# Another order of work in the attention of an attention and two mixture-of-experts kernel, 32-column logits, weights loaded in order of use

## The chip, the cores and the metric

The kernel runs on one core of a Trainium2 chip. The metric is the device time of one execution in microseconds; lower is better. A run before gives the median of three executions.

## The reference, cut to what matters

Local attention in a band of seven keys plus attention over averages of four tokens, then a soft mixture of experts (every slot is a softmax over all tokens), then a top-2 mixture. Only the first two are touched by the change.

```python
B, H, S, D = 4, 8, 576, 64                       # attention, factor 4
q_d, k_d, v_d = means over 4 tokens of q, k, v
out_up = repeat(softmax(q_d @ k_d.T / 8) @ v_d, 4 times along S)
scores = where(|i - j| < 4, q @ k.T / 8, -1e9)
x = out_up + softmax(scores) @ v                 # -> (2304, 512)

logits = x @ phi                                 # 2304 x 32, 8 experts of 4 slots
d = softmax of logits over the tokens
slot_input = d.T @ x                             # 32 x 512
slot_out[e] = relu(slot_input[e] @ w1[e]) @ w2[e]   # w1 512x1024, w2 1024x512, fp32
x = (softmax of logits over the slots) @ slot_out
# then a noisy top-2 mixture of 8 experts on x
```

## The kernel before

**Attention (to 164 us of the trace).** The work is cut into 16 units, a unit being one batch and two heads. It is software-pipelined by hand: the loop over `p` from -1 to 14 runs through the names of `SEQ` (L21) once per period, and each name is a function with an offset, so that a period holds the scores of one unit, the outputs of the unit before it, the logits of the one before that and the loads of the next. On every engine the instructions stand in just this order; nothing reorders them. After the loop `TSEQ` (L23) does the last unit and the softmax of the slots. In a period TensorE does, with the name in `SEQ` ahead: `S` band scores (L285 adds the mask with one bf16 matmul, L289 twenty 64x35 matmuls), `CP` transposes of the probabilities (L375), `SD` the scores of averages (L300), `CD` their transposes (L386), `A0`/`A1` transposes of the next unit's k and q (L231), `VD` averages of v (L268, L272), `DP` band output (L414), `EP` transposes of the output (L441, L443), `LG` logits (L463 and L465, the second one 64-column matmul for the last 64 tokens), `DD` output of the averages (L421). Every fp32 matmul shows as two records in the trace.

PSUM is read by ScalarE (ACT) or VectorE (DVE): `cp` (L216) takes DVE for the names in `ON_V`, ACT for the others. `a0j`/`a1hj` are k and q of the next unit, `pig` the transposed band probabilities (tile `PT`), `d0`/`d1` those of the averages (`PdT`), `v0`/`v1` the averaged values (`Vd`), `x0`/`x1` the band output of even and odd groups (`xT`), `k0`/`k1` its transposes (`xK`). `XA` (L433) adds the output of the averages, which stands in the same PSUM bank as the odd groups that `x1` reads. GpSimd (POOL) averages k (`KD`) and half of q (`DQ0`, L249 and L251); DVE sums the other half (`DQ1`, L245). POOL also normalises `P` and `Ed` (`P0`, `P1`, `DM`).

**Soft experts (164 to 199 us).** `hidden(e)` (L795) multiplies the slots by w1[e], `hidden_t` (L807) transposes the result by two full transposes, `second(e)` (L817) multiplies by w2[e]. The sixteen 2 MB matrices come over SP's queue (L101), each as two halves of four 256 KB or two 512 KB transfers: eight during attention (`W` issues one half a period, two in the first), three in the tail (`R2`), and the last five into ring slots that come free as the first ones are used. They are loaded in the order of their numbers, 0 (w1[0]), 1 (w2[0]), 2 (w1[1]) and so on.

Behind that stand the routing (to 215 us) and the top-2 mixture (to 492 us), which the change leaves alone. `hot(n)` (L543) issues n bf16 matmuls of 128x512 whose result nobody reads; `H2` and `H1` in `TSEQ` call it.

Of the kernel before, what the change touches and what calls it, by code (L numbers as in the profile page):

```python
# [18 lines left out]
SEQ = """S SK CP EP01 ld EP10 M EP00 ST SD CD z EP11 ED0 EL SS MD A0 ED1 EX a00 W a01 SU SU_ A1 P1 a100 a101  # L19
a110 a111 P0 KD DQ0 VD z DP V0 V1 DQ1 DX EP LG DD x1 LA lV x0 X1 SE RD DM X0 XA""".split()  # L20
TSEQ = """S:15 CP:14 W EP01:14 EP00:14 SD:15 M:15 EL:15 EP10:14 EX:15 EP11:14 CD:14 ED0:14 MD:15 SU:15 VD:14 DP:14 V0:14 V1:14 EP:13  # L21
# [12 lines left out]
N2 = 3  # L34


@with_exitstack
def attn_moe_moe_kernel(ctx: ExitStack, tc: tile.TileContext, q, k, v, moe_phi, moe_w1, moe_w2,
# [51 lines left out]
    phi4 = const.tile([128, 4, 4 * NS], F32, name="phi4")  # L90
    wgn = const.tile([128, 4, 2 * E], F32, name="wgn")

    def wload(src, kk, pool=ringa, names=("wr", "wr")):

        n = kk // 2
        ts = [pool.tile([128, 2048], F32, name=nm).rearrange("p (k f) -> p k f", k=n) for nm in names]
        sv = src.rearrange("(k p) f -> p k f", p=128)

        def go(i, eng=nc.sync):
            for k in range(n):  # L100
                eng.dma_start(out=ts[i][:, k:k + 1], in_=sv[:, n * i + k:n * i + k + 1])  # L101
        return lambda k: ts[k // n][:, k % n], [lambda i=i, **k: go(i, **k) for i in range(len(names))]
# [12 lines left out]
    with ExitStack() as tctx:  # L115
# [34 lines left out]
        P = a2.tile([128, NG, 64], F32, name="P")  # L150
        Vs = [(a1, a2)[i].tile([128, 5, 2, D], F32, name=f"V{i}") for i in range(2)]
# [27 lines left out]
        LD, VQ, KD, DQ, SD, SS, PD, PL, XL, XT, XK = ({} for _ in range(11))  # L179
# [81 lines left out]
        def v_pe(u):  # L261
# [12 lines left out]
            VQ[u] = (None, wk.tile([128, 2, 128], F32, name="Vd", bufs=1))  # L274

        def v_evac(u, i):
            xl, Vd = XL[u], VQ[u][1]
            if i:
                cp("v1", Vd[0:16, 1].rearrange("p (h d) -> p h d", h=2), xl[0:16, :, 434:498])
            else:  # L280
                cp("v0", Vd[:, 0], xl[:, 0, 290:418])

        def b_s(u):
            s = ps.tile([128, 512], F32, name="S")
            nc.tensor.matmul(s[:, 0:NG * KW], idb, mask.rearrange("p g k -> p (g k)"), start=True, stop=True)  # L285
# [6 lines left out]
            SS[u] = s  # L292
# [87 lines left out]
        def c_d(u):  # L380
# [8 lines left out]
            PdT = wk.tile([128, 2, 2, 144], F32, name="PdT", bufs=1)  # L389
            CT[u, 1] = (PdT, tt)  # L390
# [8 lines left out]
        def c_ed(u, kb):  # L399
            PdT, tt = CT[u, 1]  # L400
# [36 lines left out]
        def e_pe(u):  # L437
# [21 lines left out]
        def logit_pe(u, t2=None):  # L459
            xT, kk = XT[u], u % 4  # L460
            L = (ET_[u][1] if t2 is None else t2)[:, 128:320]
            for t in range(4):
                nc.tensor.matmul(L[32 * t:32 * t + 32, 0:128], phi4[:, kk, 0:NS], xT[:, 128 * t:128 * t + 128],  # L463
                                 start=True, stop=True, skip_group_check=True)
            nc.tensor.matmul(L[:, 128:192], phi4[:, kk], xT[:, 512:576], start=True, stop=True, skip_group_check=True)  # L465
# [79 lines left out]
        def ok(u):  # L545
# [8 lines left out]
              "DX": (soft_d2, 0, ()), "RD": (soft_d3, 0, ()), "DM": (soft_dm, 0, ()), "CP": (c_p, 1, ()),  # L554
# [23 lines left out]
        for i in range(NPRE):  # L578
            mload(i, ringa if i < 3 else ringb)
# [6 lines left out]
        for p in range(-1, NU - 1):  # L586
            if p == 0:
                nc.sync.dma_start(out=phi4[:, :, 0:NS], in_=moe_phi.rearrange("(k p) s -> p k s", p=128))
# [6 lines left out]
            for nm in SEQ:  # L595
# [66 lines left out]
        def slot_in():  # L662
            t = tp()
            for kk in range(4):
# [6 lines left out]
              "LG:15": lambda: logit_pe(NU - 1, tp()), "W": flush}  # L671
# [43 lines left out]
    with ExitStack() as mctx:  # L715
# [4 lines left out]
        for i in range(NPRE + N2, 2 * E):  # L720
            mload(i, ringa if i < NPRE + N2 + 3 else ringb)
# [79 lines left out]
        def hidden_t(e):  # L801
# [3 lines left out]
            ht_ = ps.tile([128, 2, 4, NS], F32, name="ht", bufs=1)  # L805
            for c in range(2):
                nc.tensor.transpose(ht_[:, c].rearrange("p j s -> p (j s)"), hs_[:, 128 * c:128 * c + 128], idf)  # L807
            nc.vector.tensor_scalar(hz[e][:, :, :, SPE * e:SPE * e + SPE], ht_[:, :, :, SPE * e:SPE * e + SPE],
                                    0.0, None, op0=ALU.max)
# [593 lines left out]
```

## Time and profile before

| what | us |
|---|---|
| runs, median of three | 496.54 (495.12, 496.54, 497.39) |
| the profiled execution's own time | 494.55 |
| its span in the trace | 492.7 |
| of that: start, before the first full period | 0 to 24.7 |
| thirteen periods, the regular ones of 8.3 to 8.8, those with a batch's slots of 10 | 24.7 to 141.6 |
| last unit and slots' softmax | 141.6 to 164.4 |
| soft experts | 164.4 to 198.8 |
| routing and top-2 mixture | 198.8 to 492.7 |

The profiled execution is 1.85 us longer than its span and 1.99 us below the median of the runs. A sum of terms worked out in the trace is therefore a time of that execution, and the median stands about 2 us above it.

### The profile page before, as it was taken

The page shows a single profiled execution, that of the slowest core. Times are in us where ns is not written, and L with a number is a line of the kernel's source. Part 1 is how long each engine was busy: PE and PEld are TensorE (multiplying, and loading weights), DVE is VectorE, ACT ScalarE, POOL GpSimd, SP SyncE. Part 2 cuts the span into 40 slices and gives each one's busy share as a digit, 9 for nine tenths or more (in the row PEclk, how much of TensorE's full clock was granted, in tenths as well). Part 3 has the DMA queues.
Part 4 walks back from the last instruction along what each step waited for, and adds up shares of the span by engine and source line. Part 5 has one row for each costly group of instructions (what it writes and reads, how often), then busy time and mean ns, then how long its engine had stood idle before and what let it go on. Part 6 is the DMA issues. An engine that isn't in the chain of part 4 may idle for free.

```text
span 492.7 us, 12033 instructions
## 1 busy us (share of the span) xinstructions
PE 470.2 (95%) x4569; PEld 355.9 (72%) x4569; DVE 277.4 (56%) x720; ACT 263.4 (53%) x698; POOL 199.2 (40%) x289
## 2 busy tenths in 40 slices
PE   5999999899998999899999999999999999999993
PEld 4688877777875543467787787887887887878882
DVE  7878877777875321696579545273462544624300
ACT  2567766666775021486365465483664746727410
POOL 5565636536540100166566677422222221222222
PEclk9999999999999799999999999999999999999997
DMA  9999998989979599999988744699958856333333
GB/s 160 278 243 214 233 221 192 242 216 202 265 239 345 171 393 399 389 346 338 365 258 228 224 75 76 150 363 297 275 72 229 216 128 154 43 45 43 45 43 46
DMA packets 108423, 104.16 MB, mean 211 GB/s; under 512 B 68170, under 2 KB 78090, under 8 KB 108362
## 3 DMA queue, kind: packets, MB, share of 16 engines
q1 hardware_dynamic: 101450, 90.50, 61.2%
q0 software_dynamic: 6912, 12.85, 16.6%
q8 instruction: 38, 0.62, 0.5%
q14 instruction: 23, 0.19, 0.1%
HBM read 83.60 MB, written 19.73 MB: 210 GB/s over the span
## 4 chain that ended last, share of the span: by engine, by line
PE 73%; issue 9%; DMA 7%; DVE 3%; POOL 2%; ACT 2%; POOLq 2%; SPq 0%; ACTq 0%; DVEq 0%
PE y L1054 34%; DMA wr<-in_moe_w_dram 5%; PE S L289 4%; PE t L231 3%; PE gx L871 3%; PE xl L421 3%; PE Sd L300 3%; PE xl L414 2%; PE t L375 2%; PE xl L268 2%; PE t L441 2%; PE h L1034 2%; PE t L386 2%; POOL out_dram L1073 2%; POOLq L1079 1%
## 5 line engine op out<-in xcount | busy, mean ns | idle before, releaser
L1054 PE MATMUL y<-whi,hl 128*128 128x512 f32 x320 | 127.3, 398 | 0.0
L1054 PE MATMUL y<-whi,hh 128*128 128x512 f32 x320 | 126.7, 396 | 0.4 <-ACT hh L1035 0.4
L1054 PE MATMUL y<-wlo,hh 128*128 128x512 f32 x320 | 126.5, 395 | 0.0
L1073 POOL DMA_INDIRECT out_dram<-ys,idx x40 | 64.5, 1612 | 107.9 <-ACT ys L1065 56.3
L1065 ACT ACTIVATE ys<-y,gt 128x512 f32<-128x512 f32 x40 | 27.4, 686 | 82.4 <-issue 46.9
L1026 DVE TENSOR_TENSOR wlo<-wr,whi 128x512 fp32r<-128x512 f32 x64 | 42.0, 692 | 50.3 <-ACT whi L1023 49.9
L1054 PEld LDWEIGHTS y<-wlo,hh 128*128 128x128 f32 x320 | 60.1, 188 | 12.9 <-issue 1.0
L1054 PEld LDWEIGHTS y<-whi,hl 128*128 128x128 f32 x320 | 60.1, 188 | 12.3 <-issue 2.1
L1054 PEld LDWEIGHTS y<-whi,hh 128*128 128x128 f32 x320 | 60.2, 188 | 11.8 <-ACT hh L1035 0.6
L333 POOL TENSOR_TENSOR P<-El,su 64x350 f32<-64x350 f32 x31 | 23.9, 772 | 59.7 <-DVE su L326 38.3
L1036 DVE SCALAR_TENSOR_TENSOR hl<-h,hh 128x256 fp32r<-128x256 f32 (+1 forms) x64 | 31.3, 489 | 16.0 <-ACT hh L1035 14.7
L1000 POOL DMA_INDIRECT tab<-stk,pos x36 | 35.6, 990 | 11.5 <-issue 10.7
L1036 DVE SCALAR_TENSOR_TENSOR hl<-gx,hh 128x256 fp32r<-128x256 f32 (+1 forms) x64 | 31.2, 487 | 10.7 <-ACT hh L1035 9.1
L1023 ACT ACTIVATE whi<-wr 128x512 fp32r<-128x512 f32 x64 | 36.9, 625 | 0.2
L1035 ACT ACTIVATE hh<-gx 128x256 fp32r<-128x256 f32 (+1 forms) x64 | 28.1, 439 | 15.0 <-PE gx L1034 12.5
L1035 ACT ACTIVATE hh<-h 128x256 fp32r<-128x256 f32 (+1 forms) x64 | 28.0, 437 | 12.5 <-PE h L1034 10.2
L1072 POOL MEMSET spacer<- 1x1 f32 x40 | 13.6, 340 | 41.6 <-issue 41.6
L219 ACT ACTIVATE PT<-t 64x256 f32<-64x256 f32 (+1 forms) x50 | 20.6, 417 | 13.5 <-PE t L375 12.7
L919 DVE TENSOR_TENSOR oh<-iot,R 128x256 fp32r<-128x256 f32 (+2 forms) x50 | 20.3, 439 | 11.4 <-PE xs L937 9.6
L231 PE MATMUL t<-idf,ld 96*128 96x96 f32 x192 | 21.1, 259 | 4.9 <-DMA ld<-in_k_dram 4.3
L219 ACT ACTIVATE xT<-xl 128x290 f32<-128x290 f32 x32 | 11.5, 411 | 26.2 <-PE xl L421 24.1
L289 PE MATMUL S<-K,Q 128*64 128x35 f32 x640 | 23.1, 231 | 2.2 <-issue 1.4
(301 smaller groups left out, 837.8 us busy)
## 6 DMA issues: line engine op xcount, KB each, us to landing
wr<-in_moe_w_dram SPq DMA_DIRECT2D x120, 256.0 KB, 5.6
wr<-in_moe_w_dram SPq DMA_DIRECT2D x56, 512.0 KB, 7.1
out_dram<-zero SPq DMA_DIRECT2D x20, 256.0 KB, 3.4
V<-in_v_dram SPq DMA_DIRECT2D x62, 80.0 KB, 5.2
ld<-in_k_dram SPq DMA_DIRECT2D x32, 144.0 KB, 4.7
ld<-in_q_dram SPq DMA_DIRECT2D x32, 144.0 KB, 4.4
XT<-tab SPq DMA_DIRECT2D x5, 320.0 KB, 5.6
tab<-zero SPq DMA_DIRECT2D x6, 256.0 KB, 4.8
```

The lines of the kernel that those rows point to most:

```text
L219: nc.scalar.activation(dst, src, AF.Copy)
L231: nc.tensor.transpose(t[:, 96 * c:96 * c + 96], ld[:, i, 3 * j + c].rearrange("p h d -> p (h d)"), idf[0:96, 0:96])
L289: nc.tensor.matmul(s[64 * a:64 * a + 64, KW * g:KW * g + KW], Q[:, c0:c0 + 32].rearrange("p i h -> p (i h)"), K[:, c0:c0 + KW], start=Fals ...
L333: eng.tensor_tensor(P[as_, :, HQ * a:HQ * a + KW], El[as_], su[as_, :, None].to_broadcast([64, NG, KW]), op=ALU.mult)
L1000: st = nc.gpsimd.indirect_dma_start(out=tab, out_offset=bass.IndirectOffsetOnAxis(ap=pos[:, c, i:i + 1], axis=0), in_=stk[:, i].bitcast(F3 ...
L1023: nc.scalar.activation(whi[:, kk], wb(kk), AF.Copy)
L1026: eng.tensor_tensor(wlo[:, kk], wb(kk), whi[:, kk].bitcast(F32), op=ALU.subtract)
L1035: nc.scalar.activation(hh[:, f], h, AF.Relu)
L1036: nc.vector.scalar_tensor_tensor(hl[:, f], h, 0.0, hh[:, f].bitcast(F32), op0=ALU.max, op1=ALU.subtract)
L1054: nc.tensor.matmul(y, l[:, kk, ts_], r_[:, kk], start=(m == 0), stop=(m == 23))
L1065: nc.scalar.activation(ys, YS.pop((e, ti)), AF.Copy, scale=gt[:, ti:ti + 1])
L1073: st = nc.gpsimd.indirect_dma_start(out=out, out_offset=bass.IndirectOffsetOnAxis(ap=idx[:, ti:ti + 1], axis=0), in_=ys, in_offset=None, c ...
```

## The change

- `SEQ` is another order, and `DM` works one unit later. The logits' second part becomes four 32-column matmuls like the first (so `phi4`, the copies of phi side by side, goes), and in the loop they are written into the bank of the scores (`SB`) instead of the transposes' bank.
- The mask's matmul becomes two of 64 columns. `Vd` and `PdT` are kept over the units with their second half zeroed, so that all four matmuls of `DD` take 128 rows.
- `ON_V` has other names, `DQ1` is done on POOL but for the last unit, and two `H2` (four spinning matmuls) and some other places in `TSEQ` are new.
- The sixteen matrices are loaded in `ORDW`, the order in which they are used; one half a period throughout; the last one (number 15) in another order of its quarters, the rows of `second`'s first pass first. `hidden_t` is eight matmuls of 32 columns.

```diff
-SEQ = """S SK CP EP01 ld EP10 M EP00 ST SD CD z EP11 ED0 EL SS MD A0 ED1 EX a00 W a01 SU SU_ A1 P1 a100 a101
-a110 a111 P0 KD DQ0 VD z DP V0 V1 DQ1 DX EP LG DD x1 LA lV x0 X1 SE RD DM X0 XA""".split()
+SEQ = """S ld DM M A0 a00 a01 A1 a110 a101 a100 EL SD a111 SK ST CP MD VD EP11 SS EP01 EP00 V0 EP10 V1 SU_ KD LG LA EX CD
+DQ1 W EP DP lV ED0 DX x1 ED1 DD x0 X0 X1 DQ0 SE SU P0 RD P1 XA""".split()
...
-LA:15 SE:3 X1:14 MT M4 SK:2 X1:15 SS:3 ST:3 MB R2 QW QS UA DN UB H1 SI H2 SK:3""".split()
+LA:15 SE:3 X1:14 SK:2 H2 MT M4 X1:15 SS:3 H2 ST:3 MB R2 QW QS UA DN UB H1 SI H2 SK:3""".split()
...
-ON_V = ['a110', 'a111', 'p00', 'v0', 'v1']
+ON_V = ['p11', 'k1', 'd1', 'a100', 'v0']
...
-NW = [2] + [1] * 14
+NW = [1] * 15
...
+ORDW = (0, 2, 1, 4, 3, 6, 5, 8, 7, 10, 9, 12, 11, 14, 13, 15)
...
-            if h:
+            if h and u == NU - 1:
                 return nc.vector.tensor_reduce(out=Dq[hs, :, h], in_=Q[hs, 0:576, h].rearrange(
...
-            nc.tensor.matmul(s[:, 0:NG * KW], idb, mask.rearrange("p g k -> p (g k)"), start=True, stop=True)
+            for a in range(2):
+                as_ = slice(64 * a, 64 * a + 64)
+                nc.tensor.matmul(s[as_, 0:NG * KW], idb[:, as_], mask.rearrange("p g k -> p (g k)"), start=True, stop=True,
+                                 skip_group_check=True)
...
-            xl, PdT, Vd = XL[u], CT[u, 1][0], VQ.pop(u)[1]
-            for kb, n in enumerate((128, 16)):
+            xl = XL[u]
+            for kb in range(2):
                 for h in range(2):
-                    nc.tensor.matmul(xl[64 * h:64 * h + 64, 1, 290:434], Vd[0:n, kb, 64 * h:64 * h + 64], PdT[0:n, kb, h],
+                    nc.tensor.matmul(xl[64 * h:64 * h + 64, 1, 290:434], Vd[:, kb, 64 * h:64 * h + 64], PdT[:, kb, h],
...
-            L = (ET_[u][1] if t2 is None else t2)[:, 128:320]
+            L = SB[u + 2][:, 0:192] if not TAIL else ET_[u][1][:, 128:320] if u in ET_ else tp()[:, 0:192]
...
-            nc.tensor.matmul(L[:, 128:192], phi4[:, kk], xT[:, 512:576], start=True, stop=True, skip_group_check=True)
+            for t in range(4):
+                nc.tensor.matmul(L[32 * t:32 * t + 32, 128:192], phi[:, kk], xT[:, 512:576], start=True, stop=True,
+                                 skip_group_check=True)
...
+            if i == 2 * E - 1:
+                go = [lambda f=f, c=c: f(ks=(c, c + 2)) for c in range(2) for f in go]
...
                 if p == -1 and nm == "lV":
                     nc.gpsimd.memset(PT, 0.0)
+                    nc.gpsimd.memset(Vd[:, 1], 0.0)
+                    nc.gpsimd.memset(PdT[:, 1], 0.0)
...
             for c in range(2):
-                nc.tensor.transpose(ht_[:, c].rearrange("p j s -> p (j s)"), hs_[:, 128 * c:128 * c + 128], idf)
...
+                for j in range(4):
+                    nc.tensor.matmul(ht_[32 * j:32 * j + 32, c], hs_[:, 128 * c + 32 * j:128 * c + 32 * j + 32], own_,
+                                     start=True, stop=True, skip_group_check=True)
```

The order of TensorE's instructions in a regular period, first before. The period runs from one `S` to the next; the names are tiles, `V_133` one of the two buffers of v.

```order
L285 LDWEIGHTS idb
L285 MATMUL S<-mask,idb 128x350
L289 MATMUL S<-K,Q 64x35 x20
L375 MATMUL t<-idf,P 128x128 x5
L300 MATMUL Sd<-kd,Dq 96x144 x3
...
L414 MATMUL xl<-PT,V_133 64x58 x20
L441 MATMUL t<-idf,xT 128x128 x4
L443 MATMUL t<-idf,xT 64x128
L463 MATMUL t<-xT,phi_79 32x128 x4
L465 MATMUL t<-xT,phi_79 128x64
L421 MATMUL xl<-PdT,Vd 64x144 x4
```

The same engine and place of the changed kernel:

```order
L289 MATMUL S<-mask,idb 64x350
L294 MATMUL S<-K,Q 64x35 x20
L234 MATMUL t<-idf,ld 128x96 x12
L305 MATMUL Sd<-kd,Dq 96x144 x3
L380 MATMUL t<-idf,P 128x128 x5
...
L467 MATMUL S<-xT,phi 32x128 x4
L470 MATMUL S<-xT,phi 32x64 x4
...
L447 MATMUL t<-idf,xT 64x128
L418 MATMUL xl<-PT,V_136 64x58 x20
L425 MATMUL xl<-PdT,Vd 64x144 x4
L289 LDWEIGHTS idb
```

The transposes of k and q now follow the scores, the logits stand in the middle, and `DD` follows the band output (`DP`, L418) at once and is the last work ahead of the next scores; its first matmul there waits for ACT, before it waited for DVE alone.

ScalarE in a regular period, before, from the transposed probabilities on:

```order
L219 ACTIVATE PT<-t 64x3x128
L219 ACTIVATE PT<-t 64x2x128 x2
L219 ACTIVATE PdT<-t 128x288
L219 ACTIVATE PdT<-t 16x288
L319 ACTIVATE El<-El 128x350
L219 ACTIVATE K<-t 128x288 x2
L219 ACTIVATE Q<-t 64x288 x2
L351 ACTIVATE Ed,sumd<-Sd,nmd 96x144 x3
L219 ACTIVATE xT<-xl 128x5x58 x2
L219 ACTIVATE xK<-t 64x128
L219 ACTIVATE xK<-t 128x4x128
```

And in the changed kernel, from k and q of the next unit on:

```order
L222 ACTIVATE K<-t 128x288 x2
L222 ACTIVATE Q<-t 64x288 x3
L222 ACTIVATE PT<-t 64x3x128 x2
L222 ACTIVATE PT<-t 64x2x128
L222 ACTIVATE Vd<-xl 16x128
L324 ACTIVATE El<-El 128x350
L222 ACTIVATE PdT<-t 128x288
L356 ACTIVATE Ed,sumd<-Sd,nmd 96x144 x3
L222 ACTIVATE xT<-xl 128x5x58 x2
L222 ACTIVATE xK<-t 128x4x128
```

The first `xT` (`x1`) stands behind everything that ACT does in the period, and `DD` now waits for it; before, `DD` stood ahead of it on TensorE.

TensorE in the last stretch of the slots' softmax, before (`ms`, `m` maxima, `LT` logits, `ET` their exponentials) and then in the changed kernel:

```order
L443 MATMUL t<-idf,xT 64x128
L633 MATMUL t<-idf,ms_150 1x128
L534 MATMUL t<-idf,LT_151 128x128
L535 MATMUL t<-idf,LT_151 64x32
L506 MATMUL t<-idf,ET 128x128
```

```order
L447 MATMUL t<-idf,xT 64x128
L540 MATMUL t<-idf,LT_153 128x128
L541 MATMUL t<-idf,LT_153 64x32
L549 LDWEIGHTS onesb
L549 MATMUL S<-onesb 128x512
...
L640 MATMUL t<-idf,ms_152 1x128
L549 LDWEIGHTS onesb
L549 MATMUL S<-onesb 128x512
...
L512 MATMUL t<-idf,ET 128x128
```

The transposes of the earlier batch's logits moved ahead of that of the maxima, and two spinning matmuls stand on either side of the latter, ahead of work that waits for DVE and ACT.

## Rows read from the trace of the kernel before

**Rows 1.** Windows: length, busy us (records) by engine, PEclk, DMA share, GB/s.
```profile
58.50:68.50 10.00, 10.00 (x174) 7.38 (x175) 8.24 (x22) 7.07 (x27) 6.02 (x10) 1.00 0.92 221
...
77.30:85.70 8.40, 8.40 (x157) 6.84 (x157) 6.50 (x17) 5.92 (x21) 4.83 (x8) 1.00 0.96 214
```
**Rows 2.** Chain that ended last, one regular period: start us, us, what.
```profile
77.28 1.29 PE S L289 x40
...
80.50 1.20 PE t L231 x12
...
83.91 0.35 PE t L463 x8
84.27 0.37 PE t L465 x2
84.64 0.79 PE xl L421 x8
85.42 0.26 PE S L285
```
**Rows 3.** Timeline of PEld, end of that period; in brackets its idle time before.
```profile
84.20 0.30 PEld L465 LDWEIGHTS t<-xT,phi 128*128 128x128 f32 x2 [0.20 <-issue]
...
84.96 0.19 PEld L421 LDWEIGHTS xl<-PdT,Vd 16*64 16x64 f32 x4 [0.20 <-issue]
85.35 0.10 PEld L285 LDWEIGHTS <-idb 128*128 128x128 bf16 x1 [0.20 <-issue]
85.60 0.49 PEld L289 LDWEIGHTS S<-K,Q 128*64 128x64 f32 x14 [0.16 <-issue]
```
**Rows 4.** Groups by line and form, 24.6 to 141.6 us: busy us, mean ns.
```profile
L249 POOL TENSOR_TENSOR s<-Q 64x288 f32<-64x288 f32 x14 | 13.2, 942 | 1.1
...
L245 DVE TENSOR_REDUCE Dq<-Q 64x144 f32<-64x576 f32 x13 | 9.8, 750 | 0.4
L219 ACT ACTIVATE xT<-xl 128x290 f32<-128x290 f32 x27 | 9.7, 411 | 24.2 <-PE xl L421 22.1 <-DVE rd L359 2.1
L219 ACT ACTIVATE Q<-t 64x288 f32<-64x288 f32 x26 | 9.3, 409 | 2.2 <-PE t L231 2.2
...
L219 ACT ACTIVATE xK<-t 128x512 f32<-128x512 f32 x12 | 7.1, 589 | 0.0
...
L251 POOL TENSOR_TENSOR Dq<-s 64x144 f32<-64x144 f32 x14 | 5.9, 419 | 1.1
```
**Rows 5.** Chain that ended last, tail of the attention and start of the experts.
```profile
153.08 0.73 ACT xT L219 x2
...
158.17 0.64 PE t L519 x8
...
159.46 1.01 PE t L519 x8
...
163.13 0.85 PE S L543 x2
...
164.44 3.62 PE hp L795 x48
...
168.42 1.05 PE hp L795 x16
```
**Rows 6.** Windows of 4 us around it, columns as in rows 1.
```profile
160.00:164.00 4.00, 4.00 (x24) 2.43 (x16) 1.15 (x4) 0.00 (x0) 2.04 (x21) 0.50 0.51 208
164.00:168.00 4.00, 4.00 (x51) 1.91 (x50) 0.49 (x2) 0.38 (x1) 0.00 (x0) 0.72 0.12 22
```
**Rows 7.** The same chain, end of the experts.
```profile
190.83 6.00 DMA wr<-in_moe_w_dram
...
196.87 1.90 PE yacc L817 x10
...
199.48 0.31 PE hp L847 x16
```
**Rows 8.** SP's waits, 140 to 202 us: us, times, longest.
```profile
SPq L101 <- PE hp L795: 10.9, 5, 9.5
```

More of the change, by code (lines that the diff above doesn't have):

```diff
@@ L88, in attn_moe_moe_kernel @@
     fills = [t[r:min(r + 128, t.shape[0])] for t in (tabz, out) for r in range(0, t.shape[0], 128)]
-    phi4 = const.tile([128, 4, 4 * NS], F32, name="phi4")
+    phi = const.tile([128, 4, NS], F32, name="phi")
     wgn = const.tile([128, 4, 2 * E], F32, name="wgn")
@@ L97, in wload, with go @@
         sv = src.rearrange("(k p) f -> p k f", p=128)
-        def go(i, eng=nc.sync):
-            for k in range(n):
+        def go(i, eng=nc.sync, ks=range(n)):
+            for k in ks:
                 eng.dma_start(out=ts[i][:, k:k + 1], in_=sv[:, n * i + k:n * i + k + 1])
@@ L150, in attn_moe_moe_kernel @@
         P = a2.tile([128, NG, 64], F32, name="P")
+        PdT = a2.tile([128, 2, 2, 144], F32, name="PdT")
+        Vd = a2.tile([128, 2, 128], F32, name="Vd")
         Vs = [(a1, a2)[i].tile([128, 5, 2, D], F32, name=f"V{i}") for i in range(2)]
@@ L177, in tp @@
             return ps.tile([128, 512], F32, name="t", bufs=4)
-        LD, VQ, KD, DQ, SD, SS, PD, PL, XL, XT, XK = ({} for _ in range(11))
+        LD, KD, DQ, SD, SS, SB, PD, PL, XL, XT, XK = ({} for _ in range(11))
         def load(u):
@@ L291, in b_s @@
                                      start=False, stop=True, skip_group_check=True)
-            SS[u] = s
+            SS[u] = SB[u] = s
         def b_d(u):
@@ L388, in c_d @@
                 tt.append(t)
-            PdT = wk.tile([128, 2, 2, 144], F32, name="PdT", bufs=1)
-            CT[u, 1] = (PdT, tt)
+            CT[u, 1] = tt
         def c_ep(u, i, g2):
@@ L399, in c_ed @@
         def c_ed(u, kb):
-            PdT, tt = CT[u, 1]
+            tt = CT[u, 1]
             n = (128, 16)[kb]
@@ L444, in e_pe, with e_evac @@
             ET_[u] = (t, t2)
-            if u % 4 == 0:
+        def e_evac(u, i):
+            if u // 4 not in XK:
                 XK[u // 4] = xp.tile([128, 5, 4, 128], F32, name="xK", bufs=1)
-        def e_evac(u, i):
             t = ET_[u][i]
@@ L578, in attn_moe_moe_kernel @@
         for i in range(NPRE):
-            mload(i, ringa if i < 3 else ringb)
+            mload(ORDW[i], ringa if i < 3 else ringb)
         small = [(wgn[:, :, E * i:E * i + E], w.rearrange("(k p) e -> p k e", p=128))
@@ L587, in attn_moe_moe_kernel @@
             if p == 0:
-                nc.sync.dma_start(out=phi4[:, :, 0:NS], in_=moe_phi.rearrange("(k p) s -> p k s", p=128))
+                nc.sync.dma_start(out=phi, in_=moe_phi.rearrange("(k p) s -> p k s", p=128))
             if p >= 5 and small:
@@ L720, in attn_moe_moe_kernel @@
         for i in range(NPRE + N2, 2 * E):
-            mload(i, ringa if i < NPRE + N2 + 3 else ringb)
+            mload(ORDW[i], ringa if i < NPRE + N2 + 3 else ringb)
         flush()
@@ L804, in hidden_t @@
             nc.gpsimd.memset(hz[e], 0.0)
-            ht_ = ps.tile([128, 2, 4, NS], F32, name="ht", bufs=1)
+            ht_ = ps.tile([128, 2, 4, SPE], F32, name="ht", bufs=1)
+            own_ = idf.rearrange("p (j s) -> p j s", j=4)[:, :, SPE * e:SPE * e + SPE]
             for c in range(2):
-                nc.tensor.transpose(ht_[:, c].rearrange("p j s -> p (j s)"), hs_[:, 128 * c:128 * c + 128], idf)
-            nc.vector.tensor_scalar(hz[e][:, :, :, SPE * e:SPE * e + SPE], ht_[:, :, :, SPE * e:SPE * e + SPE],
-                                    0.0, None, op0=ALU.max)
+                for j in range(4):
+                    nc.tensor.matmul(ht_[32 * j:32 * j + 32, c], hs_[:, 128 * c + 32 * j:128 * c + 32 * j + 32], own_,
+                                     start=True, stop=True, skip_group_check=True)
+            nc.vector.tensor_scalar(hz[e][:, :, :, SPE * e:SPE * e + SPE], ht_, 0.0, None, op0=ALU.max)
         def second(e, mid=None):
```

18 lines of the change are left out of this document (7 added, 11 removed).

## The prediction

> **What bounds the kernel now.** I read the windows by period first. In a regular period of 8.40 us TensorE is busy for 8.40, DVE for 6.50, ACT 5.92, POOL 4.83; in one with a batch's slots TensorE is busy for all of 10.00 [rows 1]. So in the thirteen periods only what shortens TensorE's row of work counts, or a new wait in it. The chain of one regular period shows the pieces that the change touches: the scores 1.29, the transposes of k and q 1.20, the two parts of the logits .35 and .37, `DD` .79, the mask .26 [rows 2]. The weight loads tell what some of these are made of: ahead of the logits' second part, of `DD`'s 16-row half and of the mask stands .20 each with no releaser, and .16 ahead of the scores, each time the tile shape changes [rows 3].
>
> In the tail the chain goes through DVE and ACT, then TensorE alone: the same eight matmuls take .64 at 158.17 and 1.01 at 159.46 [rows 5], and the windows give the clock, .50 from 160 to 164 and .72 from 164 to 168, with a DMA share of .12 in the latter [rows 6]. That is 1.2 GHz in place of 2.4, after a stretch in which TensorE waited again and again. The experts end on DMA: 6.00 us of waiting for the last matrix but one half, then ten records of 1.90 [rows 7], and SP had waited 9.5 us for the first `hidden` before it could issue these loads [rows 8].
>
> **Part by part.** *TensorE's work in a period.* The logits' second part: its .37 holds the .20 of shape change. In its place stand eight records of 64 columns in 32-column tiles, in the shape of the part ahead. Sixteen small records of 32-column tiles took .31 [rows 7], eight of 128 columns .35 [rows 2]; bounds .16 and .35. It is nearest to the first, since four column tiles run side by side: .17, saving .20 (bounds .02 to .21). `DD` and mask, 1.05 together: all three shape changes in and behind them go, .56 [rows 3], but the mask has a second weight load (.10, as its first [rows 3]) and `DD`'s padded half has eight times the rows to load, which I put at another .1. Saved .37, bounds 0 and .56. Together .57, so TensorE's own work falls from 8.40 to 7.83.
>
> The Trainium skill ("TensorEngine Tiling (Array Packing)", Performance Considerations, Instruction Overhead) says that a matmul has about 60 cycles of overhead and that tiling a small dimension gains nothing. As an estimate from that page, four matmuls of 64 columns would each cost what the one did and the saving would be nil, .2 us a period less. The .31 for sixteen records speaks against it.
>
> *The new wait.* In the order of instructions `DD` comes directly behind the band output and now waits for `x1` on ACT, which reads the same PSUM bank. `x1` can't start before the band output ends. It takes .411 [rows 4], and two handovers of some .04 (an "issue" piece between engines in the chain is .02 to .04; two `xT` and nothing else took .73 [rows 5]). So TensorE stands .50 in each period with nothing else to do, where before `DD` needed no such thing; behind `DD` the next mask and scores are queued, and behind these all of k, q, maxima and exponentials. 7.83 + .50 = 8.33.
>
> The skill's "PSUM — Partial Sum Buffer" (PSUM bank collisions raise a hardware error) has it that two engines must be kept apart in one bank and quadrant even at different columns. Rows of before can't show that; it is why this wait can't simply fall away.
>
> *ACT's loop.* ACT hands two small evacuations to DVE and gets one of Q (.409 [rows 4]) and a small one back, so it stays near 5.92 of 8.3. But `x1` now closes a loop. From the end of `x1`: `DD` and mask .68, scores 1.29, the first three transposes of k .30, then ACT's whole list without `x0` and `xK`, which fill the time until then (5.92 - .37 - .59 = 4.96 [rows 1, 4, 5]): 7.2. With five or so handovers and waits for DVE inside (`p10` behind `p11`, `V1` behind `v0`, `El` behind the maximum) I get about 8.2; with every mean duration in full in place of the overlapped ones, 8.9. So it is nearly as long as TensorE's 8.33, and I take 8.3, not the longer of the two to the hundredth: -.10 in each of thirteen, **-1.3**. Bounds: 8.05 (the pause covers the shape changes that are left) and 8.9, so -4.5 to +6.5.
>
> *POOL.* `DQ1` moves there: .942 + .419 [rows 4] on 4.83 makes 6.2 of 8.3, and DVE is rid of .750 [rows 4]. Hidden in a full period, as the averaged scores come a period later. In the first units it isn't: POOL has nothing to hide it behind, and the periods there are chains. I put **+.6**, bounds 0 and 1.4 (one whole `DQ1`).
>
> *Tail.* Three logits, two `DD` and a mask: -.9; the four spins, which stand ahead of work that waits for DVE and ACT in any case, delay it by some .25: **-.65**, bounds -1 and 0.
>
> *Clock.* The two `H2` fill the stretch with waits ahead of the fall. If TensorE stays at 2.4 GHz: the 5.0 us from 159.46 to 164.44 shrink. Their first piece went .64 to 1.01, a ratio of 1.6 [rows 5], so 1.9 at least; at 2, 2.5. I take 2.4. `hidden(0)` and the first part of the next, 48 records in 3.62, would be 3.15 by the 16 in 1.05 [rows 5]; .6 with what lies between. **-3.0**, bounds 0 and -3.4.
>
> *Experts.* SP waited 10.9 us for `hidden` in five waits, 9.5 of it in one [rows 8]. The first wait stays; in the order of use the second load goes into the matrix of `hidden(1)`, not into that of `second(0)`, which comes later. So of the other 1.4 us some 1.0 goes, and as DMA ends the stage, its end moves as much. The last matrix: now four of the five matmuls of 1.90 [rows 7] need not wait for the last piece; but the pieces follow each other at some .65 (256 KB, where the wait for a 2 MB matrix was 6.00 us [rows 7]), so .6 of it. **-1.6**, bounds -.4 and -3. The smaller `hidden_t` lies in TensorE's waits for DMA and gives nothing; if loads weren't the bound it would be worth some .1 each. The half matrix less in the first period goes into the tail, where DMA has room (share .51 [rows 6]): 0.
>
> Sum: -1.3 + .6 - .65 - 3.0 - 1.6 = -5.95. On the profiled execution's 494.55 that is 488.6; the median of the runs stands 2.0 above it, so **490.6**.
>
> **Rivals.** *B: the clock falls anyway*, later or at the same place; four spins are 1.7 us of TensorE at half clock by the row of two in .85 [rows 5], and the waits behind `ST` (ACT and DVE) stay as they are. For it: spins already there from 160.5 on didn't keep it up. Against: these come after the fall. Then -2.95: 493.6.
>
> *C: slower, through `x1`.* If ACT's loop is 8.8 in place of 8.3, TensorE stands .9 a period ahead of `DD`. 13 × .5 more gives +.55 in all: 497.1; without the clock 500.1. It decides from a period of 8.76 on (the other terms, -4.65, spread over thirteen, above 8.40). For it: ACT's list is in order, and `Ed`'s three exponentials stand straight ahead of `x1`. Against: ACT has 2.4 us a period to spare.
>
> *D: the pause is cheap.* TensorE's queue holds its loads ready, and `x1` starts per half of the bank: period 7.9, -6.5 in place of -1.3, 485.4.
>
> *E: the four small logits cost what the one did*, eight records of 64 columns taking the .35 of eight of 128 [rows 2]: no saving there, +.2 × 13 if TensorE's own work is the longer loop, 493.2. The row of small records leaves it .05. This is how it would go by the skill's rule on overhead, above.
>
> **Chances.** The forecast .47 (its own range 486 to 494), B .22 and E .05 (491 to 496), C .14 (495 to 501), D .12 (483 to 488). Half a per cent, 2.5 us, is about what a measurement of this kernel can tell from no change: faster is below 494.06, slower above 499.02. Faster: nearly all of the forecast (.45) and D (.12), some .6 of B and E (.15), none of C: .72. Slower: a bit under half of C, .06. Same .22. The range of 484.5 to 498 leaves out the lower third of D and the upper third of C, with the ends of the unknown costs beyond.
>
> **What would show it.** In a period: TensorE idle some .5 ahead of `DD`'s first matmul, released by ACT's `xT`; no gap without a releaser between `DD`, mask and scores; the logits' second part under .2; period 8.2 to 8.4. Tail: PEclk 1.00 in all windows from 156 to 168, `hidden(0)`'s records at .066 each. Experts: last records behind the DMA two to four, loads without a gap from the first on. It would be wrong above all if the idle time ahead of `DD` were near 1 us, or if other engines' waits opened elsewhere in the period, for which a wholly new order gives many places.

## The result, and the profile after

The changed kernel takes 497.19 us (median of twelve runs, 495.61 to 499.18), the kernel before 495.12 in twelve (490.99 to 500.69); the ratio is 1.0067, 95% interval 1.0043 to 1.0092. Ratios compare only executions in the faster of the chip's two states, so the 500.69 is not in it. I had forecast 490.6 and a gain; it is a loss, of 2.1 us by the medians and 3.3 by the ratio. The profiled execution took 496.9, its span is 495.1.

These are the ends of the stages in both traces in us, read off TensorE's timeline: the start of the mask's matmul of the third and of the last unit's scores, of the first `hidden`, of the first transpose behind the experts (`ct`), and the end.

| stage | before: ends at, lasts | after: ends at, lasts | difference | forecast |
|---|---|---|---|---|
| start | 24.40, 24.40 | 26.81, 26.81 | +2.41 | +0.6 |
| thirteen periods | 141.28, 116.88 | 146.56, 119.75 | +2.87 | -1.3 |
| last unit, slots' softmax | 164.37, 23.09 | 167.73, 21.17 | -1.92 | -3.05 |
| experts | 198.71, 34.34 | 200.97, 33.24 | -1.10 | -2.2 |
| the rest | 492.68, 293.97 | 495.12, 294.15 | +0.18 | 0 |
| sum | | | +2.44 | -5.95 |

(The forecast's clock term, -3.0, stands here with 2.4 in the slots' softmax and .6 in the experts.)

One period of the changed kernel on TensorE, in place of [rows 2 and 3]; the bracket is the idle time before a row and what ended it:

```profile
53.75 0.71 PE L425 MATMUL xl<-PdT,Vd 128*64 128x144 f32 x8 [1.21 <-ACT xT L222]
54.29 0.32 PE L289 MATMUL S<-mask,idb 128*64 128x350 bf16 x2
54.44 1.31 PE L294 MATMUL S<-K,Q 128*64 128x35 f32 x40
...
58.92 0.36 PE L470 MATMUL S<-xT,phi 128*32 128x64 f32 x8
...
60.67 0.81 PE L418 MATMUL xl<-PT,V 64*64 64x58 f32 x40
62.69 0.71 PE L425 MATMUL xl<-PdT,Vd 128*64 128x144 f32 x8 [1.21 <-ACT xT L222]
```

The reader sees one idle time only, ahead of `DD`, released by ScalarE's `xT`, and a pitch of 62.69 - 53.75 = 8.94 us. TensorE's own work is 8.94 - 1.21 = 7.73. The wait is the same in nine of the thirteen periods to within .02; in three with slots it is .58 to .70, as TensorE has more to do before, and in one 1.06. One of the three with slots, where ScalarE comes to `x1` .12 behind the end of the band output (71.80), works on it for .41 and lets `DD` go .05 later:

```profile
70.99 0.81 PE L418 MATMUL xl<-PT,V 64*64 64x58 f32 x40
71.92 0.41 ACT L222 ACTIVATE xT<-xl 128x290 f32<-128x290 f32 x1
72.38 0.71 PE L425 MATMUL xl<-PdT,Vd 128*64 128x144 f32 x8 [0.58 <-ACT xT L222]
```

ScalarE, DVE and POOL in that period:

```profile
54.51 0.41 ACT L222 ACTIVATE xT<-xl 128x290 f32<-128x290 f32 x1 [0.81 <-PE xl L425]
...
56.24 0.71 ACT L222 ACTIVATE K<-t 128x288 f32<-128x288 f32 x2 [0.83 <-PE t L234]
56.98 1.36 ACT L222 ACTIVATE Q<-t 64x288 f32<-64x288 f32 x3
58.23 0.98 ACT L222 ACTIVATE PT<-t 64x384 f32<-64x384 f32 x2
60.01 0.38 ACT L222 ACTIVATE PT<-t 64x256 f32<-64x256 f32 x1 [0.80 <-DVE PT L224]
60.33 0.27 ACT L222 ACTIVATE Vd<-xl 16x128 f32<-16x128 f32 x1
60.51 0.48 ACT L324 ACTIVATE El<-El 128x350 f32<-128x350 f32 x1
60.89 0.38 ACT L222 ACTIVATE PdT<-t 128x288 f32<-128x288 f32 x1
61.18 0.36 ACT L356 ACTIVATE Ed<-Sd,nmd 96x144 f32<-96x144 f32 x1
...
62.25 0.39 ACT L222 ACTIVATE xT<-xl 128x290 f32<-128x290 f32 x1
```

```profile
58.32 0.59 DVE L344 TENSOR_REDUCE md<-Sd 96x3 f32<-96x432 f32 x1
58.94 0.52 DVE L347 TENSOR_SCALAR nmd<-md 96x3 f32<-96x3 f32 x1
59.49 0.43 DVE L224 COPY PT<-t 64x256 f32<-64x256 f32 x1
```

```profile
58.48 0.95 POOL L252 TENSOR_TENSOR s<-Q 64x288 f32<-64x288 f32 x1 [0.28 <-ACT Q L222]
```

They close the loop that sets the 8.94, told here along ScalarE's row: from `DD` at 53.75 to the first K 2.49; K, Q and PT in a row 2.97; .80 of waiting for DVE's `p11`; from there to the end of `x1` at 62.64, 2.63; .05 to `DD`. The .80 is DVE's row: from its copy of Q at 57.52 to the end of `v0` at 60.24 it never pauses for more than .03. ScalarE's `Vd` (`V1`) at 60.33 comes just ahead of the band output (L418 at 60.67; where TensorE shows a wait ahead of L418, in five places, `V1` ends it), and behind it in ScalarE's row stand `El`, `PdT`, three `Ed` and only then `x1`. So `x1` ends 2.04 behind `V1`, the band output some .8, whatever came before. Of the 1.21, .77 is ScalarE still at this row (61.48 to 62.25), .39 is `x1` and .05 the way to `DD`.

The whole stretch of periods by engine, before and after (length, busy us, granted clock, DMA share, GB/s):

```profile
24.40:141.30 116.90, 115.36 (x2050) 91.33 (x2048) 92.57 (x245) 80.15 (x278) 64.35 (x95) 1.00 0.95 226
```

```profile
26.80:146.60 119.80, 104.63 (x2144) 90.92 (x2141) 85.69 (x230) 87.52 (x279) 79.62 (x115) 1.00 0.85 212
```

TensorE's busy time did fall, by 10.7 us, more than I had counted (13 × .57); all of it and 2.9 more became waiting.

### The profile page after: what moved, and what is told of

Read it like the earlier page. It is cut to its first block, busy times and chain, and to the rows that moved or that the text cites. A ratio compares the mean times of both kernels' runs of the same rounds, so it can differ in the third digit from the quotient of the medians.

```text
span 495.1 us, 12518 instructions
## 1 busy us (share of the span) xinstructions
PE 458.5 (93%) x4797; PEld 358.4 (72%) x4797; DVE 270.1 (55%) x702; ACT 272.3 (55%) x700; POOL 220.5 (45%) x321
## 4 chain that ended last, share of the span: by engine, by line
PE 47%; issue 4%; DVE 1%; POOLq 1%; ACT 1%; POOL 1%; DVEq 0%
PE y L1063 39%; PE gx L880 3%; PE h L1043 2%; PE gx L1043 2%; POOLq L1088 1%; DVE hl L1045 1%; PE xs L946 1%; POOL out_dram L1082 1%; PE xs L1024 1%; PE xs L943 0%; ACT hh L1044 0%; DVE wlo L1035 0%; ACT ys L1074 0%; PE gx L960 0%; ACT whi L1032 0%
## 5 line engine op out<-in xcount | busy, mean ns | idle before, releaser
L1063 PEld LDWEIGHTS y<-whi,hh 128*128 128x128 f32 x320 | 60.2, 188 | 11.8 <-ACT hh L1044 0.6
L1045 DVE SCALAR_TENSOR_TENSOR hl<-gx,hh 128x256 fp32r<-128x256 f32 (+1 forms) x64 | 31.2, 488 | 10.7 <-ACT hh L1044 8.2
L252 POOL TENSOR_TENSOR s<-Q 64x288 f32<-64x288 f32 x31 | 29.3, 946 | 6.4 <-ACT Q L222 3.0
L222 ACT ACTIVATE PT<-t 64x384 f32<-64x384 f32 (+1 forms) x50 | 22.0, 443 | 12.4 <-DVE PT L224 8.6
L425 PE MATMUL xl<-PdT,Vd 128*64 128x144 f32 x128 | 11.4, 298 | 15.9 <-ACT xT L222 15.2
```

The costliest lines, as they stand in the source:

```text
L222: nc.scalar.activation(dst, src, AF.Copy)
L252: nc.gpsimd.tensor_tensor(q2, q4[:, :, 0:2], q4[:, :, 2:4], op=ALU.add)
L1045: nc.vector.scalar_tensor_tensor(hl[:, f], h, 0.0, hh[:, f].bitcast(F32), op0=ALU.max, op1=ALU.subtract)
L1063: nc.tensor.matmul(y, l[:, kk, ts_], r_[:, kk], start=(m == 0), stop=(m == 23))
```

## The experiments

For each: what is changed against the kernel after (or before, where it says so). Medians are of ten runs each, but for four in the one without spins and two in the one with half the weights; ratios are to runs of before on the same chip, with 95% intervals.

**DD first.** `x1` behind `DD` again, so the wait is gone.

```diff
-EP DP lV ED0 DX x1 ED1 DD x0
+EP DP lV ED0 DX ED1 DD x1 x0
```

> The changed kernel with one thing undone: in the order of a period the output of the averages (DD) stands ahead of x1 again, so DD no longer waits for ScalarE's read of the bank. Theory (the period of 8.94 us is TensorE's own 7.73 and a wait of 1.21 for x1): the period falls to 7.7 to 7.9, no idle time ahead of DD, 13 periods give -13 to -15 us against the changed kernel's 497.2: 482 to 485. Rival (ScalarE's list as a whole, or POOL with its 6.3 us, is the bound and only shows at x1): the wait moves to another matmul, the period stays at 8.6 or more, 493 or more.

496.10 us, 1.0009 (.9972 to 1.0047): half of the theory holds. The wait ahead of `DD` is gone and undisturbed periods take 7.64 to 7.84, but the last scores start at 143.41, only 3 us earlier than after, 1.7 of it in the start. TensorE's waits from 24 to 142 us, and the windows of periods:

```profile
PE t L234 <- DMA ld<-in_q_dram: 6.7, 5, 2.0
PE t L234 <- DMA ld<-in_k_dram: 0.8, 1, 0.8
```

```profile
25.10:143.40 118.30, 109.08 (x2142) 95.05 (x2140) 85.77 (x230) 86.91 (x283) 80.60 (x117) 0.96 0.91 216
```

TensorE now waits for q and k, 7.5 us in six waits, and the clock, 1.00 before and after, is .96: it falls to 1.2 GHz around such waits (88 to 95 us and 136 to 139, with waits of 1.80 and 2.03). Of the 118.3 us the waits for loads are 7.5, and TensorE's busy time is 4.5 longer than in the changed kernel (109.08 and 104.63). The runs' mean granted clock is .982 here and .990 in the changed kernel. Neither theory nor rival came out as I wrote them: a second bound stands right behind the first, the loads of q and k.

**x1 on DVE.** ScalarE is spared `x1`; `DD` still waits for it.

```diff
-ON_V = ['p11', 'k1', 'd1', 'a100', 'v0']
+ON_V = ['p11', 'k1', 'd1', 'a100', 'v0', 'x1']
-DX x1 ED1 DD
+DX ED1 x1 DD
```

> The changed kernel with x1 read by DVE (behind d1) in place of ScalarE; DD still waits for x1. Theory (DD waits 1.21 because x1 stands on ScalarE behind El, PdT and the three Ed, which all come after V1, which releases DP; x1 itself is only .4 of it): TensorE's wait ahead of DD falls to about .5, the regular period from 8.94 to 8.2 or 8.3, as long as the loads of q and k keep up; 487 to 491, and later if TensorE then waits for q and k, as it does in the run in which DD stands first. Rival (any read of the bank between DP and DD costs as much): wait ahead of DD stays over 1 us, same time as the changed kernel.

496.03, 1.0027 (.9991 to 1.0063). The wait falls to .80, not to .5, the period to 8.67:

```profile
59.32 0.81 PE L418 MATMUL xl<-PT,V 64*64 64x58 f32 x40
60.92 0.71 PE L425 MATMUL xl<-PdT,Vd 128*64 128x144 f32 x8 [0.79 <-DVE xT L224]
```

```profile
60.32 0.46 DVE L224 COPY xT<-xl 128x290 f32<-128x290 f32 x1 [0.81 <-PE xl L418]
```

DVE had been idle for .81 and starts `x1` .19 after the band output's end (60.13), needs .46, and `DD` starts .14 after that. So .79 is the price of this wait with DVE reading and free: 7.73 + .79 = 8.52, which is above the 8.40 of before. In this kernel another .22 of waiting for ScalarE's `PT` comes on top. On ScalarE the handovers are shorter: `x0` starts .05 behind the end of `DD` (54.46 to 54.51), `DD` .05 behind the end of `x1` (62.64 to 62.69), and the wait was .58 in the period with slots above. As an estimate from these rows, a ScalarE that is free when the band output ends would make it .05 + .39 + .05, some .5; no run has that.

**p11 first.** DVE's `p11` ahead of `md` and `nmd`, so that ScalarE needn't wait .80 ahead of `p10`.

```diff
-CP MD VD EP11 SS EP01
+CP EP11 VD MD SS EP01
```

> The changed kernel with DVE's p11 (the transposed probabilities' second part) ahead of the maxima of the averages, so that ScalarE's p10, which waits for p11, and all of its list behind p10 up to x1 come earlier. Theory (x1 is late because p10 stands .80 us waiting for p11, which stands behind md .59 and nmd .52 on DVE): ScalarE's gap of .80 goes, TensorE's wait ahead of DD falls from 1.21 to .5 (x1 itself and handovers), period 8.2 to 8.3, 488 to 490. Rival (x1 is late because ScalarE's list is too long): the wait ahead of DD stays near 1.2, same time as the changed kernel.

496.88, 1.0055 (1.0016 to 1.0094), period 8.86, wait 1.23: the rival's numbers, though not by its reason. ScalarE's idle time went one instruction on:

```profile
60.22 0.27 ACT L222 ACTIVATE Vd<-xl 16x128 f32<-16x128 f32 x1 [0.77 <-DVE Vd L224]
```

`V1` waits for `v0`, which stands behind the same `md` and `nmd` in DVE's row, and that row as a whole, from its copy of Q to the end of `v0`, is 2.63 in place of 2.72, as the period is .08 shorter. And as `V1` releases the band output too, getting it earlier would move both ends of the wait.

**DQ1 on DVE** in all units.

```diff
-            if h and u == NU - 1:
+            if h:
```

> The changed kernel with DQ1 back on DVE in all units. Theory: nmd on DVE takes .17 again in place of .52, which is the time that POOL's sum (.95) needs to end, so p11, p10 and x1 come .35 earlier and the period is 8.6 to 8.7; the start (to the second full period) loses about 1.5 us of its 2.4; 491 to 493. Rival (POOL has no part in it, and DVE pays .75 more): the period stays at 8.9 or grows, 496 or more.

494.01, 1.0003 (.9973 to 1.0033). `nmd` takes .31, the period 8.74, and the second scores of the start come at 14.92 in place of 16.94. Of the theory the direction is shown in both places, of the period's .35 only .20, and the total misses the 491 to 493. DVE's row from Q to `v0` is 2.51 here, .21 shorter than in the changed kernel, and the period is shorter by as much: the loop runs through this row. With this alone undone the changed kernel is level with the one before; the same holds for DD first and for `x1` on DVE. The start of the changed kernel shows the averages' scores waiting for POOL (before, they followed the scores at 10.70 without a wait); the second row is that of the run with half the weights, in which POOL does `DQ1` too:

```profile
13.42 1.75 PE L305 MATMUL Sd<-kd,Dq 128*96 128x144 f32 x6 [0.67 <-POOL Dq L254]
```

```profile
13.23 0.98 PE L305 MATMUL Sd<-kd,Dq 128*96 128x144 f32 x6 [0.77 <-POOL Dq L254]
```

The latter's second scores start at 15.13, nearly as early as with `DQ1` on DVE (14.92). So of the 2.0 between 16.94 and 14.92 most isn't the wait for POOL: the same six matmuls take 1.75 or .98 (.92 with `DQ1` on DVE), the four spins behind them 1.91 or 1.03. In the kernel before the six take 1.75 too, but earlier, and its spins 1.03. The seven traces with `DQ1` on POOL and 1.75 at this place start the second scores at 16.62 to 17.20. Whether the wait for POOL keeps TensorE slow in these is not shown.

**Forms of matmul alone, on the kernel before**: mask in two halves, `DD` padded, logits in 32 columns, all other things as before.

```diff
+            for a in range(2):
+                as_ = slice(64 * a, 64 * a + 64)
+                nc.tensor.matmul(s[as_, 0:NG * KW], idb[:, as_], mask..., start=True, stop=True, skip_group_check=True)
...
-            for kb, n in enumerate((128, 16)):
+            for kb in range(2):
...
+            for t in range(4):
+                nc.tensor.matmul(L[32 * t:32 * t + 32, 128:192], phi4[:, kk, 0:NS], xT[:, 512:576], ...)
```

> The kernel before with only the matmul forms changed: mask in two halves of 64 columns, DD padded to 128 rows, logits' second part in 32-column tiles; order and engines as before. Theory (TensorE's row of work bounds the periods of before, and these forms save the gaps of shape changes): the period falls from 8.40 by .4 to .6, 13 periods and the tail give -5 to -8 us, 487 to 490. Rival (the time is given back, as another engine's loop stands right behind TensorE): period 8.2 or more, -2 us or less.

491.51, .992 (.9882 to .9958): faster. The rows that answer to [rows 2 and 3]:

```profile
39.83 0.29 PE L469 MATMUL t<-xT,phi 128*32 128x64 f32 x8
40.05 0.71 PE L424 MATMUL xl<-PdT,Vd 128*64 128x144 f32 x8
40.59 0.32 PE L288 MATMUL S<-mask,idb 128*64 128x350 bf16 x2
40.74 1.31 PE L293 MATMUL S<-K,Q 128*64 128x35 f32 x40
...
47.82 0.29 PE L469 MATMUL t<-xT,phi 128*32 128x64 f32 x8
48.05 0.71 PE L424 MATMUL xl<-PdT,Vd 128*64 128x144 f32 x8
48.59 0.32 PE L288 MATMUL S<-mask,idb 128*64 128x350 bf16 x2
```

The period is 8.00: .40 saved by these forms, where .57 was forecast. The logits' second part goes from its row's start to the next in .22 (39.83 to 40.05), `DD` and mask with the way to the scores in .69. That is .15 and .36 less than the .37 and 1.05 of [rows 2], where I had .20 and .37. Eight records in .22, where two with their change of shape had taken .37, go against my estimate that four small matmuls save nothing. I had made that estimate from the Trainium skill ("TensorEngine Tiling (Array Packing)", Instruction Overhead), whose figure of some 60 cycles a matmul is not contradicted: .22 for eight records is 66 cycles each at 2.4 GHz. Over the thirteen periods it gained only 1.6 us (115.26, with 2.2 us of idle time that has no releaser, where the kernel before has one such piece of 1.4). The profiled execution, 494.8, is 3.3 above the median of its runs, and its span of 492.9 shows no gain on the 492.7 of before; where the other runs gain their 4 us this trace can't tell. The window of its periods:

```profile
24.30:139.50 115.20, 109.38 (x2142) 92.68 (x2138) 91.70 (x244) 80.40 (x278) 64.27 (x94) 1.00 0.99 225
```

The DMA engines' share is .99, and yet TensorE waits for no load in it.

**Loads of q and k ahead of v's** on SP's queue, with DD first; and the same with DQ1 on DVE for the first two units.

```diff
-"ld": (load, -2, ())
+"ld": (load, -3, ())
-EP DP lV ED0 DX ED1 DD x1 x0
+EP DP ld lV ED0 DX ED1 DD x1 x0
+        load(1)
```

> The changed kernel with DD ahead of x1, and the loads of the next q and k issued ahead of those of v on SP's queue (one unit further ahead in program order), so that they no longer stand behind v's, which wait for the end of the band output. Theory (with DD first the periods without a late load took 7.6 to 7.8 us, and the rest of the time was lost in waits for q and k, behind v on SP): waits for q and k go, regular period 7.8, S15 at 136 to 139 in place of 143.4, total 488 to 492. Rival (the DMA engines themselves are at their limit at 8.4 us a period): other waits for loads take their place, S15 at 142 or later.

> As the run with early loads, and DQ1 on DVE for the first two units. Theory (DQ1 on POOL costs the start about 2 us, as the second S came at 14.9 in place of 16.9 with DQ1 on DVE): S2 at 23 to 24, a further 1.5 to 2 us less than the run with early loads alone. Rival (the start is made up in the periods, which wait for loads): same time as that run.

498.98, 1.005 (1.0015 to 1.0084), and 498.69, 1.0077 (1.0047 to 1.0106): both slower, as the rival had it. Only the second's trace is read here: start 23.77 us as expected, first periods of 7.65, and then the waits again, with a clock of .94:

```profile
PE t L234 <- DMA ld<-in_q_dram: 6.2, 7, 1.9
PE t L234 <- DMA ld<-in_k_dram: 3.9, 5, 1.1
```

```profile
23.80:147.60 123.80, 111.65 (x2144) 97.11 (x2140) 85.80 (x230) 87.19 (x282) 80.40 (x117) 0.94 0.95 211
```

**Half the weights in the attention**, with DD first: this asks whether the amount of loading or the order of the queue delays q and k.

```diff
-NW = [1] * 15
+NW = [1, 0] * 7 + [1]
```

> The changed kernel with DD ahead of x1 and only every second period's half matrix issued in the attention, the other seven at the tail's W. Theory (with x1's wait gone, the DMA engines' throughput is the next bound of the periods: 1.9 MB a period, share .91 to .99): waits for q and k go, regular period 7.6 to 7.8 all through, S15 at 131 to 136, no fall of the clock within the periods; the total doesn't gain as much, since the matrices left over are loaded later at some 390 GB/s: 488 to 494. Rival (SP's in-order queue, where q and k stand behind v's wait for the band output, delays the loads whatever their number): the waits for q stay, S15 at 141 or later.

The last scores start at 132.55, eleven us earlier than with all the weights, 1.1 of it in the start; periods of 7.65 to 7.8 where nothing is waited for; the waits for q and k sink from 7.5 to 3.8 us:

```profile
PE t L234 <- DMA ld<-in_q_dram: 2.7, 4, 0.7
...
PE t L234 <- DMA ld<-in_k_dram: 1.1, 1, 1.1
```

```profile
24.03:132.55 108.52, 104.17 (x2143) 91.04 (x2139) 83.30 (x229) 86.65 (x282) 80.72 (x117) 1.00 0.77 177
```

Of the 9.8 us that the thirteen periods lose, half is TensorE's busy time (109.1 to 104.2, at a clock of 1.00 in place of .96), half is idle time. So the amount of loading it is, with a remainder that may be the queue's order. That the DMA engines' throughput is the limit is not shown: SP's own issuing of the weights falls too, from 24.3 to 11.8 us of these periods by its rows in the traces, and with the new forms on the kernel before a share of .99 went with no wait for a load. The total, 500.83 (1.0125, 1.001 to 1.024, of two runs), is worse and not the 488 to 494 expected: the matrices left over are then waited for, and the experts take 50 us in place of 33.

**Two halves in the first period**, as before the change.

```diff
-NW = [1] * 15
+NW = [2] + [1] * 14
```

> The changed kernel with two half matrices issued in the first period again (NW as before), so that one half less is left for the tail. Theory (the experts end when the DMA queue has moved the matrices left at the attention's end, at some 390 GB/s without a gap from 150 us on, and early in the attention the queue has room: share .65 to .8 between 24 and 32 us): the experts end 2 to 2.7 us earlier (1 MB), 494.5 to 495.5. Rival (DMA has no room in the attention, q and k come later): S15 moves by as much, no change.

498.14, 1.0083 (1.0045 to 1.0121). The experts end at 201.30 as in the changed kernel; my theory on DMA falls. The first `hidden` starts at 167.94 and the experts take 33.36 from there: by now they are a row of TensorE's work, as the next run shows.

**Order of the matrices alone, on the kernel before** (with the last one in quarters).

```diff
+ORDW = (0, 2, 1, 4, 3, 6, 5, 8, 7, 10, 9, 12, 11, 14, 13, 15)
-mload(i, ...)
+mload(ORDW[i], ...)
```

> The kernel before with the order of the matrices by use and the last one in quarters alone. Theory (from the first hidden on the experts take 34.2 to 34.3 us in every kernel with the old order and 32.1 to 33.4 in those with the new one): ct minus first hidden falls from 34.3 to 32 to 33.4, and the total by 1 to 2 us: 493 to 494.5 where before is 495. Rival (the shorter stage of the changed kernels comes from their later start, as the tail's loads are then less far ahead): 34 us and no change.

495.16, .9981 (.9936 to 1.0027): no change that can be told. The experts' 33.58 us end on TensorE, where before they ended on DMA [rows 7]. The longest pieces of the chain:

```profile
182.69 1.73 PE hp L798 x32
184.42 0.86 PE yacc L820 x8
185.65 1.00 PE yacc L820 x8
186.64 1.73 PE hp L798 x32
188.37 0.86 PE yacc L820 x8
189.60 4.56 PE yacc L820 x24
```

An expert takes 3.95 us of TensorE (182.69 to 186.64), eight of them 31.6. So a better order could give no more than a part of the 34.34 - 31.6.

**Spins**, taken out of the changed kernel and put alone into the one before.

```diff
-LA:15 SE:3 X1:14 SK:2 H2 MT M4 X1:15 SS:3 H2 ST:3 ...
+LA:15 SE:3 X1:14 SK:2 MT M4 X1:15 SS:3 ST:3 ...
```

> The changed kernel without the two H2 ahead of MT and ST. Theory (they keep the clock at 2.4 GHz through the slots' softmax, but the experts' end hangs on DMA and not on TensorE, so it gains nothing): the granted clock falls to 1.2 for some 7 us about 155 to 170 us in the profile, hidden(0) starts 1 to 3 us later, the experts end at 201 as in the changed kernel, total within 1 us of 497.2. Rival (my forecast: the clock is worth 3 us): 499 to 501.

> The kernel before with the two H2 (and SK:2 ahead of them) alone. Theory (in the kernel before the tail's loads are through at 162 and the next ones wait for hidden(0), so there TensorE's pace in the tail does count): no fall of the clock between 155 and 170, hidden(0) starts some 2 us earlier, the experts end 2 to 3 us earlier: 491.5 to 493 against 494.5. Rival (the clock falls a little later anyway, or the spins cost what they save): within 1 us of before.

497.82, 1.0109 (1.0019 to 1.0199) without them, and 493.96, .9984 (.9942 to 1.0027) with them in the kernel before. Two windows of the changed kernel without spins:

```profile
160.00:164.00 4.00, 3.00 (x44) 1.88 (x43) 3.28 (x13) 2.28 (x9) 0.00 (x0) 1.00 1.03 403
...
214.00:222.00 8.00, 7.64 (x27) 5.71 (x27) 6.95 (x16) 5.20 (x13) 5.68 (x7) 0.64 1.05 354
```

No fall in the tail, which takes 21.17 us, as with spins; the fall begins at about 216 here. In the kernel before with spins the second window has one too (.66).

**All of it but the order and the engines, on the kernel before**: forms, order of the matrices, quarters, spins.

> The kernel before with everything of the change but its order of the periods and its choice of engines: matmul forms, order of the matrices, last one in quarters, two H2. Theory (each part of the change that is not the order or the engines gains): -3 us as the forms alone gave, -1 to -2 from the matrices, spins 0 to -1: 489 to 491, faster than before and than the changed kernel. Rival (DMA takes the gains back, as the attention's loads are near their limit): 492 or more.

491.59, .9917 (.9876 to .9958): faster than both kernels, and no faster than the forms alone.

## Why the prediction was wrong, by its own steps

**The step that failed is the thirteen periods, -1.3** (measured: +2.87), and in it the new wait: I let `x1` start as the band output ends, where ScalarE was still busy with what stands ahead of it.

- *The new wait, .50.* The place was right, ahead of `DD`, released by ScalarE's `xT`, and nothing else stands on TensorE. It is 1.21, because `x1` begins .77 behind the end of the band output. The rest of it, .39 and .05, is as I had it, and so are handovers of .04 (ScalarE's are .05); they don't hold for DVE, whose .19 and .14 make it .79. With the .58 of the period with slots in every period, 7.73 + .58 = 8.31 would have been about the forecast's 8.33.
- *ACT's loop, about 8.2.* It is 8.94, at my upper bound of 8.9. The list from the first K to the end of `x1` took 5.6 of ScalarE's time, not 4.96, and .80 of waiting for DVE on top, so the loop ran through DVE's row as well. What I missed is that `V1` releases the band output and that `El`, `PdT` and `Ed` stand between `V1` and `x1`: the wait is then the difference of two lengths behind the same event (2.04 and .8), which a busy share of 5.9 in 8.3 can't show. The run with `p11` first bears this out: `p11` came earlier and the wait stayed 1.23.
- *Rival C* had this mechanism, at a chance of .14; "ACT has 2.4 us a period to spare" spoke against it and was no argument, since ScalarE is idle while TensorE and DVE are waited for. That its time, 497.1 with the clock kept, is the measured one is luck: it had +5.2 in the periods and -4.65 elsewhere, where the traces have +2.87 and -.43.
- *TensorE's own work, -.57*: right in kind; the forms alone saved .40, and with the new order it is .67 a period. (By its own terms, .56 less twice .10, the saving of `DD` and mask was .36, not .37.)
- *What I had not seen at all*: with the wait gone the loads of q and k are the next bound. The DMA engines' share was .95 in the periods of before (.92 and .96 in [rows 1]); I read it and did not ask what a shorter period would do with it. Half the weights gave 9.8 us there, half of it through TensorE's clock. So even my case D, 7.9 a period, was not to be had in this order with 1 MB of weights in each.

**The start, +.6**: +2.41, above my bound of 1.4. The first units are a chain, and POOL now does `DQ1` in it, ahead of averages' scores that wait .67 for it; with `DQ1` on DVE 1.9 of it goes (24.92 in place of 26.81). Most of that is TensorE's matmuls at nearly twice their time behind the wait, which one trace with `DQ1` on POOL does not show.

**The clock, -3.0**: mis-sized, and in part no term at all. The fall at 159.4 belongs to the one profiled execution. In the kernel before, the executions with a mean clock of .993 or more (10 of 30, 5 of 22 and 5 of 26 on three chips) have medians .9, 2.3 and 1.1 us below those of all that the ratios count: in the median the falls are worth some 1 to 2 us, not 3. Of fifteen kernels profiled, eleven with the spins had no fall in the slots' softmax and two of the four without had one; but the fall then often comes behind the experts, and the mean clock of the runs is about the same (.990 of the changed kernel, .990, .987 and .987 of before).

**The median above the profiled execution, 2.0**: three runs gave that; with twelve the median of the kernel before is 495.12, .57 above its 494.55.

**The tail, -.65**, is bounded by the two kernels without a fall there: 21.17 in the changed one, 20.96 in the kernel before with the spins. So nothing of it shows, where I had three logits, two `DD` and a mask; the variants of the changed kernel spread from 20.42 to 22.09.

**The experts, -1.6**: -1.10, of the right sign and mechanism, but ended by TensorE's own 3.95 an expert, which I never added up. (The .65 I took for a 256 KB piece isn't what its row gives either: an eighth of 6.00 is .75.)

What stays open: whether the DMA engines, SP's issuing or its order makes q and k late; why the start's matmuls run slow in most traces with `DQ1` on POOL; and why the mean clock drops with TensorE's short waits (.982 with DD first) more than with the regular 1.21 a period (.990).

## What to carry to other kernels

An engine that is idle more than a quarter of the time (ScalarE: 87.52 busy of 119.80) can still set the pace when an instruction at the end of its row releases the bound engine: add up the row between the event that releases both and the release, not the busy share. Before a saving on the bound engine is multiplied by the periods, look for what stands right behind it; here it was the loads of q and k. The DMA share alone did not tell: one order waited 7.5 us for them at .91, another not at all at .99. A clock that falls in one profiled execution is no term of a sum against the median of many: see first in how many of the runs it falls.

## What the runs showed of the hardware

- From the last matmul of a group to the read that waits for it, and from the end of a read to the matmul that waits for that: .05 and .05 on ScalarE (changed kernel, 54.46 and 62.64), .19 and .14 on DVE (`x1` on DVE, 60.13 and 60.78). The ends of matmuls are modelled in the profile.
- DVE's `nmd` on 96x3 elements takes .17 in all thirteen periods of the kernel before, where POOL does nothing at that time. In the changed kernel twelve of thirteen begin while a sum of POOL's runs, and each ends .02 or .03 behind that sum, after .20 to .87 (in the period shown 59.46 and 59.43). With `DQ1` on DVE it is .31 and with `p11` first .44 in a regular period, with the same distance to POOL's end. So DVE looks held until POOL is done; why, no run shows.
- The granted clock falls to 1.2 GHz at places that differ between executions of kernels that do the same work there: at 159.4 in the trace of before, at about 216 in the one without spins, nowhere in that of the changed kernel.
- In the start the same six matmuls took 1.75 in the changed kernel and .98 in the run with half the weights, while the column of the granted clock reads 1.00 in both.
